# Gate/up stage of a gated FNet and GEGLU kernel: T1 streams loaded ahead of h's stores, raw weights loaded later, D product behind S3 for one token pair

## The chip, the cores and the metric

One core of a Trainium2 chip runs the kernel. The metric is the device time of one execution in microseconds (us), the median of the runs shown. A run takes 1026.12 us before the change; three runs gave 1026.1, 1026.12 and 1030.14 us. The profile is that of a further execution.

## The reference

x has 2048 tokens of 640 values. One half is an FNet layer, the real part of a Fourier transform over the hidden size and then over the sequence, written as products with cosine and sine matrices. The other half is a GEGLU feed-forward layer with 1728 hidden units. A sigmoid gate mixes the two for each token. All is float32.

```python
g = sigmoid((x * gate_w).sum(-1, keepdims=True))
a = x @ dft_hid_re.T
b = x @ dft_hid_im.T
A = dft_seq_re @ a - dft_seq_im @ b
B = (gelu(x @ w_gate) * (x @ w_up)) @ w_down
out = g * A + (1 - g) * B
```

## The kernel before

**Arithmetic.** Every float32 operand is kept as a high and a low part, so one product of two tiles is three matmuls into the same PSUM bank (`mm3`, lines 101 to 103: high by high, high by low, low by high). A split is made by ScalarE (ACT) writing the high part (line 82) and VectorE (DVE) subtracting it from the raw value for the low part (line 85). A second way of making a low part exists for x in the Fourier stage: ACT writes the negative high part (line 93), and a DMA on GpSimd's queue (POOL) adds the raw value to it in memory (`left_of`, line 97).

**Seven products.** The gate/up stage works on blocks f of 128 hidden units, f = 1 to 12, and on two token pairs, tp = 0 and 1. Products of two-by-two blocks are made with seven products instead of eight: sums of weight blocks (S1 to S4, A11, A12, A22) times sums of token blocks (T1 to T4). The hidden size of x is five tiles of 128: four go into this form, and `u5`, `g5` and `D` are the weights that meet the fifth tile of x (x1 and x2 below are its two token halves). The blocks f = 5 and 6, 7 and 8, 9 and 10, 11 and 12 also form pairs, whose A11 products are themselves shared in a seven-product form over the blocks (`together`, `together_up`). From f = 7 on (`THIRD`), S1 times T1 is shared in the same way (`together_s`): it needs three combined token streams, called xs1 to xs3 here. `pair_of(f)` is 1 for the first block of a pair and 2 for the second.

**The streams.** `sums_across("xs", ...)` makes those three streams once. `loads_s` reads four raw blocks of T1 from DRAM, on the queue of SyncE (SP). `s123` is a list of five pieces of work: sums, part 1, sums, part 2, part 3. Each part splits its sum into high and low and stores both to DRAM on POOL's queue. `load_across` loads one stream back (512 KB, on POOL's queue) for each of the blocks 7, 9 and 11. `xq` and `xu` are the like streams of the other two shared products.

**Order.** The code runs inside `in_order(PE, ACT, DVE, POOL)`: each engine executes its instructions in the order in which the code issues them. `gate_up` is a generator, one for each token pair, and the loop over `step` runs a piece of one and then a piece of the other. Behind each piece `fill` takes work off the list `fills` (weight sums and splits, token sums) by a budget of costs. So DVE and ACT hold the evictions of PSUM that TensorE waits for and the preparation of later blocks in one stream each. `make_w`, `load_w`, `make_third` and `load_third` prepare and load the weights of the next block and of the next pair; `load_third` loads the raw weights called wt. POOL's queue holds h's stores as well: `keep(hA...)` on line 456 stores the hidden values of a block, four stores for each.

**The steps concerned.** In a second block from f = 8 on, `gate_up` issues S4, S2, then the D product into bank pZ, then S3 into bank pX, then `u5` times x1 into the same bank pX, which S3's values must have left first (line 675 adds them to `s5`). Line 667 adds the bank of D to `s2`. In `f == THIRD - 2`, which is 5, the raw blocks are loaded at step 4 and three pieces of `s123` are queued at the end of `fills`; the other two follow in block 6. At step 5 of a second block stream xs2 of the next block is loaded, ahead of h's stores; xs1 and xs3 are loaded inside the next block, behind them. In block 12 the first tiles of the Fourier stage (`split_xa`, `split_c`) are prepared: x's low part by DVE for the first column piece (`sp` = 0), by DMA for the next.

Of the kernel before, what the change touches and what calls it, by code (L numbers as in the profile page):

```python
# [12 lines left out]
ALU = mybir.AluOpType  # L13
# [9 lines left out]
NF = F // P  # L23
# [6 lines left out]
THIRD = 7  # L30
# [7 lines left out]
def kernel(  # L38
# [60 lines left out]
    def mm3(ps, lhs, rhs, first, last):  # L99
        (lh, ll), (rh, rl) = lhs, rhs  # L100
        nc.tensor.matmul(ps, lh, rh, start=first, stop=False, skip_group_check=True)  # L101
        nc.tensor.matmul(ps, lh, rl, start=False, stop=False, skip_group_check=True)  # L102
        nc.tensor.matmul(ps, ll, rh, start=False, stop=last, skip_group_check=True)  # L103
# [500 lines left out]
    def gate_up(f, W, B, tp, s5, s1t, xs, s4, zs):  # L604

        n = f"{f}_{tp}"
        kind = pair_of(f)  # L610
        s_kind = kind if f >= THIRD else 0
        if s_kind == 2:
            Z = zs[f][tp]
            mm3(Z, W["u5"], at(B[5], 1), False, True)
            yield 68
            nc.scalar.activation(s5, Z, AF.Copy)
            yield
        X = bank(f"pX{n}")
        if not s_kind:
            Z = bank(f"pZ{n}")  # L620
        xs[tp] = X
        x1, x2 = at(B[5], 0), at(B[5], 1)
        k, second = divmod(f - 1, 2)

        def prod(ps, a, b, first):
            for i in range(2):
                mm3(ps, W[a, i], at(B[b], i), first and i == 0, True)

        prod(X, "A11", (1, 1), True)
        yield 136  # L630
        if not kind:
            V = bank(f"pV{n}")
            nc.scalar.activation(V, X, AF.Copy)
        else:
            s1 = s1t[kind - 1, tp] if (kind, tp) != (1, 1) else None
            if s1 is not None:
                tt(s1, s1, X, op=ALU.add)
        yield
        if not kind:
            prod(V, "A12", (2, 1), False)  # L640
            mm3(V, W["g5"], x1, False, True)
            yield 204
            s1 = mtile(F32, f"s1{n}")
            nc.scalar.activation(s1, V, AF.Gelu_apprx_tanh)
            yield
        if not s_kind:
            prod(Z, "S1", "T1", True)
            mm3(Z, W["u5"], x2, False, True)
            yield 204
            nc.scalar.activation(s5, Z, AF.Copy)  # L650
            yield
        elif s_kind == 1:
            yield 0
            yield
            Z = zs[f][tp]
        else:
            prod(Z, "S4", (2, 2), False)
            yield 136
            yield
        prod(X, "S2", "T2", False)  # L660
        yield 136
        s2 = copy(X, f"s2{n}")
        yield
        mm3(Z, W["D"], x2, False, s_kind == 2)
        yield 68
        if s_kind == 2:
            tt(s2, s2, Z, op=ALU.add)
            nc.scalar.activation(s2, s2, AF.Gelu_apprx_tanh)
        if kind:
            s1 = s1t[kind - 1, tp]  # L670
            nc.scalar.activation(s1, s1, AF.Gelu_apprx_tanh)
        yield
        prod(X, "S3", "T3", False)
        yield 136
        tt(s5, s5, X, op=ALU.add)
        yield
        if s_kind != 2:
            prod(Z, "S4", (2, 2), False)
            yield 136
            tt(s2, s2, Z, op=ALU.add)  # L680
            nc.scalar.activation(s2, s2, AF.Gelu_apprx_tanh)  # L681
            yield
        if not kind:
            prod(X, "A22", "T4", False)
        mm3(X, W["u5"], x1, False, True)
        yield 68 if kind else 204
        tt(s2, s2, s5, op=ALU.mult)  # L687
        keep(hA[tp][k], 1 + 2 * second, s2)
        if kind:
            c21 = s4[kind - 1, tp]  # L690
            tt(c21, c21, X, op=ALU.add)
            tt(s1, s1, c21, op=ALU.mult)
        else:
            tt(s1, s1, X, op=ALU.mult)
        keep(hA[tp][k], 2 * second, s1)
        if k not in STORED:
            yield
            return
        if not second:
            tt(s5, s2, s1, op=ALU.subtract)  # L700
            keep(hT[tp][k], 0, s5)
            hid[tp] = s2, s5
            yield
            return
        h12, t1 = hid.pop(tp)

        def last_sums():
            tt(h12, s2, h12, op=ALU.subtract)
            keep(hT[tp][k], 2, h12)
            tt(t1, s2, t1, op=ALU.subtract)  # L710
            keep(hT[tp][k], 1, t1)

        def last_sum():
            tt(s5, s1, t1, op=ALU.subtract)
            keep(hT[tp][k], 3, s5)

        todo.extend([(122, last_sums), (61, last_sum)])
        yield
# [641 lines left out]
    with in_order(PE, ACT, DVE, POOL):  # L1360
        for f in range(1, NF):
# [10 lines left out]
                loadp()  # L1372
                fills.extend(t123)
            if f == THIRD - 1:
                fills.extend(s123[3:])
            third = kind == 1 and f >= THIRD
            if f + 1 < NF and not third:
                nxt, work = make_w(f + 1)
                if f + 1 == THIRD:
                    ws, (sums, across, highs, lows) = make_third(f + 1)  # L1380
                    work = [sums, *work[:2], across, *work[2:4], highs, work[4], lows, *work[5:]]
                if kind != 1 or f == PAIRED:
                    fills.extend(work)
            if kind == 1 and PAIRED < f < THIRD:
                fills.extend(work)
            if f == NF - 1:
                for k in range(2):
                    fetch_xn(k)
                    load_c(k)

                def made():
                    sums_made.pop(0)()

                for k in range(2):
                    fills.extend([(126, partial(split_xa, k, not k)), (122, made), (245, partial(split_c, k))])
                fills.extend([(126, partial(split_xa, 2, False)), (0, made)])
            state.update(pe=0, done=0, all=sum(c for c, _ in fills), pe_all=2450 if not kind else (2994, 1768)[kind - 1] if f < THIRD else (3198, 1496)[kind - 1])
            s5 = pair(F32, f"s5{f}")
            xs = {}
# [11 lines left out]
                more_s = together_s(f, W, ws, s5, zs, parks)  # L1411
            for k in range(4):
                run(more)
                if third and k in (1, 3):
                    load_across(f, "xs", Ts, kepts, k)
                if third and k == 2:
                    load_w(f + 1)
                    if f + 2 < NF:
                        load_third(f + 2)
            for step in range(8 if not kind else 7):  # L1420
                if third and step == 5:
                    unpark(f + 1, zs, parks)
                for tp, w in enumerate(work):
                    run(w)
                    if third:
                        if step == 0:
                            run(more_s if not tp else more)
                        if (step, tp) == (0, 1):
                            load_across(f, "xu", Tu, keptu, 1)
                            run(more_s)  # L1430
                            load_across(f, "xu", Tu, keptu, 2)
                            run(more)
                            run(more_s)
                            run(more)
                            run(more_s)
                            load_across(f, "xu", Tu, keptu, 3)
                        elif (step, tp) == (2, 0):
                            run(more_s)
                            run(more_s)
                        elif (step, tp) == (3, 0):  # L1440
                            run(more_s)
                    elif (step, tp) in ((0, 1), (1, 1)):
                        run(more)
                        if step == 0:
                            run(more)
                    if (2, 0) < (step, tp) < (6, 0):
                        run(more_up)
# [4 lines left out]
                    for k in (1, 2, 3):  # L1452
                        load_across(f + 1, "xq", Tp, keptp, k)
                if step == 5 and pair_of(f + 1) == 1 and f + 1 >= THIRD:
                    load_across(f + 1, "xs", Ts, kepts, 2)
                if f == THIRD - 2 and step == 4:
                    loads_s()
                    fills.extend(s123[:3])
                if f == THIRD - 1 and step == 5:
                    todo.extend(s4th)  # L1460
                if step == 5 and f + 2 == THIRD:
# [1 line left out]
                if third and step == 1:  # L1463
                    nxt, parts = make_w(f + 1)
                    if f + 2 < NF:
                        ws, (sums, across, highs, lows) = make_third(f + 2)
                        parts = [*parts[:3], sums, across, *parts[3:5], highs, parts[5], lows, *parts[6:]]
                    fills.extend(parts)
                    state["all"] += sum(c for c, _ in parts)
                if step == 5 and not (f + 2 >= THIRD and pair_of(f + 2) == 2):  # L1470
# [461 lines left out]
```

## Time and profile before

| what | value |
|---|---|
| runs | 1026.1, 1026.12, 1030.14 us |
| the profiled execution | 1028.07 us |
| its span in the profile | 1026.3 us |
| granted TensorE clock, mean | 0.998 |
| TensorE matmuls, busy | 1015.4 us, 99% of the span |
| VectorE busy | 832.0 us, 81% |
| ScalarE busy | 508.8 us, 50% |
| GpSimd busy | 188.6 us, 18% |
| share of TensorE in the chain that ended last | 91% |

The profile is that of one execution. Its time, 1028.07 us, holds 1.8 us outside the span. Lines of the profile name the engine, the line of the kernel and the tiles: `pX<-x05h,wa` is a matmul that reads x05h and wa and writes bank pX. `xs<-xs` is the load of a stream, from DRAM tile xs to tile xs on the chip. A wait in square brackets ahead of an arrow says how long the engine sat idle and what released it.

### The profile page before, as it was taken

Reading aid. Unit: us, or ns where it says so; the run is one execution under the profiler, and the core shown is the slowest. Engines: PE = TensorE matmul, PEld = TensorE weight load, DVE = VectorE, ACT = ScalarE, POOL = GpSimd, SP = SyncE. Lnnn points to the kernel's source line nnn. Section 1 sums busy time; section 2 is a strip of 40 time slices with the busy share of each in tenths; the row PEclk is TensorE's granted clock in tenths of the full one; section 3 lists DMA queues with packets and bytes.
Section 4 is the critical chain, followed back from the end, with each engine's and each line's share of the span. In section 5 each row is a group of like instructions: output and inputs, shape, how many; then the busy total and the mean of one; then the engine's idle time right before and its main releaser. Section 6 shows DMA issues by size and latency. Waiting matters only on the chain.

```text
span 1026.3 us, 13389 instructions
## 1 busy us (share of the span) xinstructions
PE 1015.4 (99%) x4480; PEld 835.0 (81%) x4480; DVE 832.0 (81%) x1186; ACT 508.8 (50%) x660; POOL 188.6 (18%) x329
## 2 busy tenths in 40 slices
PE   9999999999999999999999999999999999999998
PEld 7888787787878878888888888888888888888887
DVE  8987776776856778987977897679798997997796
ACT  6644445454544764442543444434637736664340
POOL 1221232314120210032004301220111011011112
PEclk9999999999999999999999999999999999999999
DMA  9566485939596996589669966979989998997856
GB/s 351 157 210 228 167 268 188 307 135 300 161 315 215 300 244 214 195 313 381 227 202 351 352 233 224 376 259 326 338 302 384 360 387 330 350 363 213 267 143 100
DMA packets 97878, 275.46 MB, mean 268 GB/s; under 512 B 13008, under 2 KB 24912, under 8 KB 97808
## 3 DMA queue, kind: packets, MB, share of 16 engines
q1 hardware_dynamic: 68640, 182.35, 50.7%
q0 software_dynamic: 28880, 92.05, 28.5%
q8 instruction: 35, 0.57, 0.2%
q14 instruction: 35, 0.29, 0.1%
q10 hardware_dynamic: 288, 0.20, 0.1%
HBM read 199.03 MB, written 66.60 MB: 259 GB/s over the span
## 4 chain that ended last, share of the span: by engine, by line
PE 91%; DVE 3%; DMA 3%; issue 2%; ACT 1%; POOL 0%; DVEq 0%; POOLq 0%; ACTq 0%
PE pX L103 6%; PE pX L101 6%; PE pX L102 6%; PE pZ L101 4%; PE pZ L102 4%; PE pZ L103 4%; PE pL L103 3%; PE pL L102 3%; PE pL L101 3%; PE pV L101 2%; PE pV L102 2%; PE pV L103 2%; PE pR L102 1%; PE pQ L102 1%; PE pY L102 1%
## 5 line engine op out<-in xcount | busy, mean ns | idle before, releaser
L82 ACT ACTIVATE ch<-csa 128x1024 fp32r<-128x1024 f32 x32 | 34.0, 1062 | 78.2 <-DVE csa L894 72.9
L85 DVE TENSOR_TENSOR cl<-cra,ch 128x1024 fp32r<-128x1024 f32 x32 | 39.1, 1222 | 24.0 <-ACT ch L82 21.8
L82 ACT ACTIVATE ch<-cra 128x1024 fp32r<-128x1024 f32 x32 | 33.9, 1059 | 46.8 <-DVE cl L85 14.2
L85 DVE TENSOR_TENSOR cl<-crb,ch 128x1024 fp32r<-128x1024 f32 x32 | 39.1, 1222 | 16.1 <-ACT ch L82 14.7
L456 POOL DMA_DIRECT2D hA<-s x48 | 26.4, 550 | 137.0 <-DVE s L687 118.4
L103 PE MATMUL pL<-ch,xal 128*128 128x512 f32 x128 | 50.1, 392 | 0.0
L102 PE MATMUL pL<-cl,xah 128*128 128x512 f32 x128 | 50.1, 391 | 0.0
L101 PE MATMUL pL<-ch,xah 128*128 128x512 f32 x128 | 48.8, 389 | 0.0
L82 ACT ACTIVATE ch<-crb 128x1024 fp32r<-128x1024 f32 x32 | 33.8, 1056 | 29.6 <-DVE cl L85 8.5
L85 DVE TENSOR_TENSOR cl<-csa,ch 128x1024 fp32r<-128x1024 f32 x32 | 39.1, 1221 | 8.4 <-ACT ch L82 6.2
L149 ACT ACTIVATE s<-pX 128x512 f32<-128x512 f32 x41 | 24.1, 596 | 40.9 <-PE pX L103 40.0
L85 DVE TENSOR_TENSOR cl<-csb,ch 128x1024 fp32r<-128x1024 f32 x32 | 39.2, 1224 | 4.2 <-ACT ch L82 3.2
L82 ACT ACTIVATE ch<-csb 128x1024 fp32r<-128x1024 f32 x32 | 34.0, 1062 | 13.9 <-DVE csb L897 5.2
L1532 POOL DMA_DIRECT2D uA<-c x8 | 4.3, 539 | 168.1 <-DVE c L1644 167.8
L103 PEld LDWEIGHTS pL<-ch,xal 128*128 128x128 f32 x128 | 24.2, 189 | 5.1
L101 PEld LDWEIGHTS pL<-ch,xah 128*128 128x128 f32 x128 | 24.0, 188 | 5.1
L102 PEld LDWEIGHTS pL<-cl,xah 128*128 128x128 f32 x128 | 24.0, 188 | 5.0
L82 ACT ACTIVATE kh<-kw 128x1024 fp32r<-128x1024 f32 x24 | 25.5, 1063 | 5.1 <-PE kL L102 4.2
L681 ACT ACTIVATE s<-s 128x512 f32<-128x512 f32 x18 | 11.3, 633 | 32.8 <-DVE s L680 32.8
L103 PE MATMUL pX<-ch,xal 128*128 128x512 f32 x64 | 25.1, 393 | 2.2 <-DMA xal<-xn 2.2
L85 DVE TENSOR_TENSOR kl<-kw,kh 128x1024 fp32r<-128x1024 f32 x18 | 21.9, 1219 | 4.4 <-ACT kh L82 4.4
L103 PE MATMUL pZ<-ch,xal 128*128 128x512 f32 x64 | 25.4, 397 | 0.0
(3759 smaller groups left out, 3508.6 us busy)
## 6 DMA issues: line engine op xcount, KB each, us to landing
cra<-in_ct SPq DMA_DIRECT2D x64, 512.0 KB, 5.0
crb<-in_ct SPq DMA_DIRECT2D x64, 512.0 KB, 5.6
kr<-hA SPq DMA_DIRECT2D x36, 512.0 KB, 7.6
hA<-s POOLq DMA_DIRECT2D x48, 256.0 KB, 3.2
ux<-uA SPq DMA_DIRECT2D x24, 512.0 KB, 7.5
ux<-uT SPq DMA_DIRECT2D x16, 512.0 KB, 6.3
hT<-s POOLq DMA_DIRECT2D x24, 256.0 KB, 3.7
xq<-xp POOLq DMA_DIRECT2D x12, 512.0 KB, 4.7
```

The costliest lines, as they stand in the source:

```text
L82: nc.scalar.activation(hi, raw, AF.Copy)
L85: nc.vector.tensor_tensor(lo, raw, hi.bitcast(F32), op=ALU.subtract)
L101: nc.tensor.matmul(ps, lh, rh, start=first, stop=False, skip_group_check=True)
L102: nc.tensor.matmul(ps, lh, rl, start=False, stop=False, skip_group_check=True)
L103: nc.tensor.matmul(ps, ll, rh, start=False, stop=last, skip_group_check=True)
L149: nc.scalar.activation(m, src, AF.Copy)
L456: nc.gpsimd.dma_start(to[:, i], src)
L681: nc.scalar.activation(s2, s2, AF.Gelu_apprx_tanh)
L1532: nc.gpsimd.dma_start(to[:, i], src)
```

## The change

1. In block 5 the raw blocks of T1 are loaded at the start, two pieces of `s123` (sums, part 1) stand ahead of the weight work, and two (sums, part 2) behind it; block 6 keeps only part 3.
2. At step 5 of blocks 6, 8 and 10 both xs2 and xs1 of the next block are loaded; inside the next block only xs3 is.
3. `load_third(f + 2)` moves from the run ahead of the steps to step (0, 1), behind the third `xu` load.
4. The weight work of blocks 7 and 9 is queued in another order.
5. In blocks 8, 10 and 12, for tp = 1, S3 and its addition are issued ahead of the D product; tp = 0 gets empty steps so that both have eight.
6. `split_xa(1)` makes the low part by DVE, as `split_xa(0)` does; its ACT negative and its DMA on POOL's queue are gone.

```diff
@@ gate_up
         s2 = copy(X, f"s2{n}")
         yield
+        if s_kind == 2 and tp:
+            yield 0
+            yield
+            prod(X, "S3", "T3", False)
+            yield 136
+            tt(s5, s5, X, op=ALU.add)
+            yield
         mm3(Z, W["D"], x2, False, s_kind == 2)
...
-        prod(X, "S3", "T3", False)
-        yield 136
-        tt(s5, s5, X, op=ALU.add)
-        yield
+        if s_kind != 2 or not tp:
+            prod(X, "S3", "T3", False)
+            yield 136
+            tt(s5, s5, X, op=ALU.add)
+            yield
+        if s_kind == 2 and not tp:
+            yield 0
+            yield
@@ the loop over f
             if f == THIRD - 1:
-                fills.extend(s123[3:])
+                fills.extend(s123[4:])
...
+            if f == THIRD - 2:
+                loads_s()
+                work = [*s123[:2], *work, *s123[2:4]]
...
-                    fills.extend([(126, partial(split_xa, k, not k)), (122, made), (245, partial(split_c, k))])
+                    fills.extend([(126, partial(split_xa, k)), (122, made), (245, partial(split_c, k))])
...
-                if third and k in (1, 3):
-                    load_across(f, "xs", Ts, kepts, k)
+                if third and k == 1:
+                    load_across(f, "xs", Ts, kepts, 3)
                 if third and k == 2:
                     load_w(f + 1)
-                    if f + 2 < NF:
-                        load_third(f + 2)
-            for step in range(8 if not kind else 7):
+            for step in range(7 if kind and not (kind == 2 and f >= THIRD) else 8):
...
                             load_across(f, "xu", Tu, keptu, 3)
+                            if f + 2 < NF:
+                                load_third(f + 2)
...
                 if step == 5 and pair_of(f + 1) == 1 and f + 1 >= THIRD:
-                    load_across(f + 1, "xs", Ts, kepts, 2)
-                if f == THIRD - 2 and step == 4:
-                    loads_s()
-                    fills.extend(s123[:3])
+                    for k in (2, 1):
+                        load_across(f + 1, "xs", Ts, kepts, k)
...
-                        parts = [*parts[:3], sums, across, *parts[3:5], highs, parts[5], lows, *parts[6:]]
+                        parts = [*parts[:5], sums, parts[5], across, parts[6], highs, lows]
```

Line numbers behind the first edit are 7 or 11 higher in the changed kernel (a load of a stream is on line 1340 instead of 1329, line 667 becomes 674, line 675 becomes 683, or 669 in the new place).

The first place is POOL's queue where block 6 ends and block 7 begins. `hA` are h's stores, the number behind `xs_` on the right is the DRAM tile of a stream: 573 is xs1, 574 is xs2, 575 is xs3. Before:

```order
L1329 DMA xs_1824<-xs_574 128x1024
L456 DMA hA_67<-s_0_1747 128x512
L456 DMA hA_67<-s_1523 128x512
L456 DMA hA_73<-s_1_1761 128x512
L456 DMA hA_73<-s_1432 128x512
L1329 DMA xs_1863<-xs_573 128x1024
L1329 DMA xs_1888<-xs_575 128x1024
```

In the changed kernel the same place of POOL's queue reads:

```order
L1340 DMA xs_1824<-xs_574 128x1024
L1340 DMA xs_1826<-xs_573 128x1024
L456 DMA hA_67<-s_0_1753 128x512
L456 DMA hA_67<-s_1539 128x512
L456 DMA hA_73<-s_1_1768 128x512
L456 DMA hA_73<-s_1440 128x512
L1340 DMA xs_1865<-xs_575 128x1024
```

The load of xs1 moved past h's four stores; xs3 is left behind them. It is the same where block 8 ends and where block 10 ends.

The second place is VectorE at the end of block 8; pZ_0 and pZ_1 are the banks of D for tp = 0 and 1, pX_0 and pX_1 those of S3. Before:

```order
L85 TENSOR_TENSOR ws9l<-ws9r,ws9h 128x1024
L667 TENSOR_TENSOR s_0_2186<-s_0_2186,pZ_0_2068 128x512
L667 TENSOR_TENSOR s_1_2197<-s_1_2197,pZ_1_2069 128x512
L675 TENSOR_TENSOR s_2124<-s_2124,pX_0_2140 128x512
L675 TENSOR_TENSOR s_2124<-s_2124,pX_1_2151 128x512
```

In the changed kernel the same place of VectorE reads:

```order
L85 TENSOR_TENSOR ws9l<-ws9r,ws9h 128x1024
L674 TENSOR_TENSOR s_0_2186<-s_0_2186,pZ_0_2068 128x512
L683 TENSOR_TENSOR s_2124<-s_2124,pX_0_2140 128x512
L669 TENSOR_TENSOR s_2124<-s_2124,pX_1_2151 128x512
L674 TENSOR_TENSOR s_1_2197<-s_1_2197,pZ_1_2069 128x512
```

The read of bank pZ_1 moved behind both reads of pX, so one operation instead of two stands between the weight split and the first read of pX. Blocks 10 and 12 have the same rows in the same change.

The third place is TensorE in block 12, ahead of `u5` times x1 into pX_0 (`x05h`, `wa`). The tiles ch, cl and xah, xal belong to the Fourier stage. Before:

```order
L103 MATMUL pX_1_2971<-xT13h,ws12l 128x512
L101 MATMUL pZ_3116<-ch_1_2966,xah_2943 128x512
L102 MATMUL pZ_3116<-cl_1_2967,xah_2943 128x512
L103 MATMUL pZ_3116<-ch_1_2966,xal_2944 128x512
L103 MATMUL pX_3114<-ch_0_3005,xal_2986 128x512
L102 MATMUL pX_3115<-cl_0_3006,xah_2985 128x512
L103 MATMUL pX_3115<-ch_0_3005,xal_2986 128x512
L102 MATMUL pL_3120<-cl_0_3006,xah_2985 128x512
L103 MATMUL pL_3120<-ch_0_3005,xal_2986 128x512
L101 MATMUL pL_3121<-ch_0_3005,xah_2985 128x512
L102 MATMUL pL_3121<-cl_0_3006,xah_2985 128x512
```

Behind these come the last row of pL_3121 and three of pZ_3117, and then `u5`. In the changed kernel TensorE's rows from D's last matmul to `u5` are:

```order
L103 MATMUL pZ_1_2879<-x15h,wa_2801 128x512
L101 MATMUL pZ_3115<-ch_1_2966,xah_2943 128x512
L102 MATMUL pZ_3115<-cl_1_2967,xah_2943 128x512
L103 MATMUL pZ_3115<-ch_1_2966,xal_2944 128x512
L102 MATMUL pX_3114<-cl_0_3005,xah_2985 128x512
L103 MATMUL pX_3114<-ch_0_3004,xal_2986 128x512
L101 MATMUL pL_3119<-ch_0_3004,xah_2985 128x512
L102 MATMUL pL_3119<-cl_0_3005,xah_2985 128x512
L103 MATMUL pL_3119<-ch_0_3004,xal_2986 128x512
L101 MATMUL pX_0_2955<-x05h,wa_2801 128x512
```

`u5` is row 1487 of TensorE's order instead of 1493, so six matmuls of the Fourier stage that stood ahead of it are now behind it. The number of matmuls is 4496 in both orders.

## The prediction

> **What bounds the kernel now.** I read the page first: its busy times and its chain.
>
> ```profile
> PE 1015.4 (99%) x4480; PEld 835.0 (81%) x4480; DVE 832.0 (81%) x1186; ACT 508.8 (50%) x660; POOL 188.6 (18%) x329
> PE 91%; DVE 3%; DMA 3%; issue 2%; ACT 1%; POOL 0%; DVEq 0%; POOLq 0%; ACTq 0%
> ```
>
> TensorE is busy for 99% of the span, and the change leaves it the same 4496 matmuls. It can therefore only win or lose TensorE's waits and stretches of a slower clock. The waits of TensorE, summed by what ended them (us in total, times, longest), come next.
>
> ```profile
> PE pX L103 <- DMA xal<-xn: 2.2, 1, 2.2
> PE pX L101 <- DVE s L675: 1.3, 2, 0.7
> PE pX L101 <- DVE s L637: 1.0, 1, 1.0
> PE pZ L101 <- ACT s L149: 1.0, 1, 1.0
> PE pZ L101 <- DMA xs<-xs: 0.9, 1, 0.9
> ```
>
> These six waits are 6.4 us, and all lie where the change works. Third, each is sized in TensorE's timeline, as the distance of two starts less a step between matmuls. The step is 0.23 us (254.35 to 254.58 below). The columns are start, duration, engine, line, operation, and in brackets the idle time.
>
> ```profile
> 178.10 0.39 PE L103 MATMUL pZ<-x15h,wa 128*128 128x512 f32 x1
> 179.49 0.50 PE L101 MATMUL pX<-xT02h,ws6h 128*128 128x512 f32 x1 [1.00 <-DVE s L637]
> 179.82 0.39 PE L102 MATMUL pX<-xT02l,ws6h 128*128 128x512 f32 x1
> ...
> 203.24 0.39 PE L103 MATMUL pH7t<-x05h,wq7l 128*128 128x512 f32 x1
> 204.56 0.47 PE L101 MATMUL pZ<-xs,wt7h 128*128 128x512 f32 x1 [0.93 <-DMA xs<-xs]
> ...
> 237.38 0.39 PE L103 MATMUL pX<-xT13h,ws8l 128*128 128x512 f32 x1
> 238.43 0.50 PE L101 MATMUL pX<-x05h,wa 128*128 128x512 f32 x1 [0.67 <-DVE s L675]
> ...
> 252.65 0.39 PE L103 MATMUL pH9t<-x05h,wq9l 128*128 128x512 f32 x1
> 254.04 0.47 PE L101 MATMUL pZ<-xs,wt9h 128*128 128x512 f32 x1 [1.00 <-ACT s L149]
> 254.35 0.40 PE L102 MATMUL pZ<-xs,wt9h 128*128 128x512 f32 x1
> 254.58 0.40 PE L103 MATMUL pZ<-xs,wt9l 128*128 128x512 f32 x1
> ...
> 358.64 0.39 PE L102 MATMUL pX<-cl,xah 128*128 128x512 f32 x1
> 361.21 0.50 PE L103 MATMUL pX<-ch,xal 128*128 128x512 f32 x1 [2.18 <-DMA xal<-xn]
> ```
>
> The step that follows a wait is longer too (179.49 to 179.82, 0.33 for 0.23), so a wait costs 0.1 more than its gap. Block 6: 1.39 less 0.23, and 0.10, is **1.26**. Block 7: 1.32 less 0.23, and 0.08, is **1.17**. Block 8: 1.05 less 0.23, and 0.1, is 0.92, and block 10 the same, as the second of the two waits on line 675. Block 9: 1.39 less 0.23, and 0.08, is **1.24**. Block 12, where x's low part is waited for: 2.57 less 0.23, and 0.1, is **2.44**. Block 9's wait is booked on ACT, but its matmul reads stream xs1 as the one in block 7 does, whose wait ended with that load; I take it for the load.
>
> Last I looked at the clock behind the longest wait. The windows table has busy times, then the granted clock, the DMA share and GB/s.
>
> ```profile
> 354.00:358.00 4.00, 4.00 (x20) 3.30 (x19) 3.50 (x6) 3.30 (x5) 0.64 (x1) 1.00 1.04 330
> ...
> 362.00:366.00 4.00, 4.00 (x12) 3.12 (x11) 3.47 (x6) 3.34 (x4) 0.87 (x1) 0.57 1.05 331
> ```
>
> From 362 to 366 the clock was 0.57, so 0.43 of 4 us, **1.7 us**, was lost on top of the wait. The same page's mean clock, 0.998 of 1026 us, leaves room for about one such stretch (2 us). The DMA share is above 1 throughout: transfers there stand in each other's way.
>
> **The change part by part.** *Streams made in block 5 (edit 1).* VectorE before, in block 5 and ahead of block 6's wait, and a piece of the chain there:
>
> ```profile
> 159.87 0.69 DVE L85 TENSOR_TENSOR wa<-wa6r,wa 128x512 fp32r<-128x512 f32 x1 [2.77 <-ACT wa L82]
> 163.56 0.69 DVE L675 TENSOR_TENSOR s<-s,pX 128x512 f32<-128x512 f32 x1 [3.00 <-PE pX L103]
> 165.60 0.69 DVE L675 TENSOR_TENSOR s<-s,pX 128x512 f32<-128x512 f32 x1 [1.35 <-PE pX L103]
> ...
> 177.55 1.28 DVE L85 TENSOR_TENSOR xs<-xs,xs 128x512 fp32r<-128x512 f32 x2
> 178.76 0.68 DVE L637 TENSOR_TENSOR s<-s,pX 128x512 f32<-128x512 f32 x1
> ...
> 174.41 2.83 DMA wt7b<-in_wf
> ```
>
> Line 637 reads the bank that S2 writes next, and stands behind the stream work, four sums and three low parts. In the new order one low part is left ahead of line 637, and six operations of 0.68 at most, 4.1 us, move into block 5, where VectorE idles 7.1 us in the three rows. In their place one operation, line 277 on the raw weights wt7a and wt7b, moves ahead of line 637. If wt7b lands as late as before, at 177.24, line 637 ends at 177.24 + 0.60 + 0.68 = 178.5, 0.2 behind S2's turn (178.10 + 0.23); otherwise well ahead of it. I take **1.26**, all of block 6's wait, with 0.3 less as the other end. The cover is block 5's idle time; without it, each 0.7 us of VectorE ahead of the evictions on line 675 would show. The four raw loads move with the work, ahead of block 6's weights on SP's queue, and the two stores of xs1 on POOL's go ahead of the `xu` loads. No row shows these waits. If the four 256 KB reads at the 330 GB/s of the windows above (3.2 us) hit a load that is just in time, they cost at most those 3.2 us; below nothing is excluded, as nothing waits there now. I take 0, since the idle rows there end on TensorE and ACT and not on a load.
>
> *xs1 ahead of h's stores (edit 2).* POOL before, and the chain's piece:
>
> ```profile
> 189.37 0.55 POOL L1329 DMA_DIRECT2D xs<-xs  x1 [0.99 <-DVE s L675]
> 194.96 0.54 POOL L456 DMA_DIRECT2D hA<-s  x1 [0.83 <-DVE s L692]
> 195.57 1.16 POOL L1329 DMA_DIRECT2D xs<-xs  x2
> 195.57 8.85 DMA xs<-xs
> 206.72 0.39 PE L101 MATMUL pH7s<-xs,wt7h 128*128 128x512 f32 x1
> ```
>
> The load of xs1 was issued at 195.57, behind stores that wait for VectorE's last results, and flew 8.85 us, to 204.42. Behind xs2 it can go at 189.37 + 0.55 = 189.92. With the same flight it lands at 198.8, and is needed at 203.24 + 0.23 = 203.47. 4.7 us of room also cover a later free buffer. So **1.17** goes, and in block 9, the same wait at the same place of its block, **1.24**. What is late next is xs3: still issued behind the stores, second of the pair at 195.57, landed at 205.0 with the same flight, used at 206.72. TensorE comes to that matmul earlier by the 1.26 and 1.17, at 204.3. Its load has no xs1 beside it now, 0.5 MB or 1.5 us at 330 GB/s, so I take 203.5 and no wait; with the old flight it is 0.7 late.
>
> *S3 before D (edit 5).* VectorE before, in block 8:
>
> ```profile
> 236.50 1.28 DVE L667 TENSOR_TENSOR s<-s,pZ 128x512 f32<-128x512 f32 x2
> 237.70 1.28 DVE L675 TENSOR_TENSOR s<-s,pX 128x512 f32<-128x512 f32 x2
> ```
>
> The matmul at 238.43 waits for the first line 675 (237.70 and 0.68). One of the two operations ahead moves behind, and they start 0.60 apart, so the wait shrinks from 0.92 to 0.32: **0.60** in block 8 and **0.60** in block 10. D's bank is read 1.2 later, but its consumers are ACT and h's stores, which nothing on TensorE awaits here.
>
> *x's low part by VectorE (edit 6), and six matmuls behind `u5`.* The rows of block 12:
>
> ```profile
> 333.97 1.04 ACT L93 ACTIVATE xal<-xn 128x1024 fp32r<-128x1024 f32 x1
> 335.99 1.23 DVE L85 TENSOR_TENSOR cl<-cra,ch 128x1024 fp32r<-128x1024 f32 x1 [3.02 <-ACT ch L82]
> 344.63 0.69 DVE L691 TENSOR_TENSOR s<-s,pX 128x512 f32<-128x512 f32 x1 [1.93 <-PE pX L103]
> 349.39 1.06 ACT L82 ACTIVATE xah<-xn 128x1024 fp32r<-128x1024 f32 x1 [3.51 <-DVE xn L860]
> 351.81 9.35 DMA xal<-xn
> ```
>
> ACT loses 1.04, VectorE gains 1.22 inside an idle 3.02: nothing on the path. One accumulating DMA of 512 KB goes. The transfer that TensorE waits for is two pieces further; its ACT work waited for VectorE (3.51), and VectorE for `u5` (1.93 idle ahead of 344.63). `u5` now stands six matmuls, 6 x 0.23 = 1.4 us, earlier. So the transfer starts at 350.4 instead of 351.81 and with 9.35 lands 1.4 earlier. Its flight should shrink by up to the 1.5 that a half megabyte takes; I count 0.6, because the share stays above 1. Of 2.44, **2.0** goes, between 1.0 (ACT's step alone) and all.
>
> *The clock.* Behind block 9's wait, 1.24, TensorE keeps the step of 0.23 (254.35 to 254.58), so a rest of 0.4 should not start a low clock: **1.7** goes. The Trainium skill's page "TensorE: Matmul & The Clock Gate", section "HAM oscillation — how this bites in real kernels", states the rule "no PE-idle gaps >~3.4µs". By it a wait of 2.18 would not have cost the clock, and the sum would lack this 1.7; the trace has the low clock right behind that wait, so I follow the trace.
>
> *Edits 3 and 4*, weight loads and pieces moved: no wait of TensorE is on them now. Between nothing and, where a moved load is late, a wait like the xs rows, 1.2; I take 0.
>
> **Sum.** 1.26 + 1.17 + 1.24 + 0.60 + 0.60 + 2.0 + 1.7 = 8.6. Against the profiled execution's own 1028.07 that is 1019.5. The runs' median is 1.95 lower; if that is the stretch of low clock missing there, the sum is 6.9 from 1026.1, 1019.2. I predict **1019.5**.
>
> **The rivals.** *Low part still late.* If the 3.51 idle moves little and the flight stays, 1.0 is won and the low clock stays: 1028.07 − 4.87 − 1.0 = **1022.2**. For it speak the DMA share above 1; against it the six matmuls.
>
> *xs1 doesn't come earlier.* If it still waits for a buffer or an earlier DMA until h's stores are out, blocks 7 and 9 keep 2.4: **1021.9**. Against it, xs2 left at 189.37 through the same queue.
>
> *The clock stays for another reason*, as by the page's rule: without the 1.7, **1021.2**.
>
> *Slower: xs3 takes xs1's place.* In blocks 7, 9 and 11 the one load left behind the stores would meet the moved raw weights on full DMA engines. At 0.7 late it gives back 0.7 in two or three blocks: 1021.0 to 1021.6. From about 2 us late on (landing past 206.3 in block 7) the low clock joins, as in block 12: 2.44 + 1.7 = 4.1 in each of three blocks, 12.4 in all, **1031.9**. The flight of 8.85 at full share speaks for it, the load's unchanged place and lighter company against.
>
> **How the numbers follow.** The sum 0.52; low part late 0.17; xs1 not earlier 0.07; clock kept 0.07; xs3 mildly late 0.09; xs3 heavily late 0.08. Low end: all of blocks 8, 10 and 12, and the median's base with the low clock in it, 1026.1 − 9.6 = 1016.5. High end: the mild cases and half of the heavy one, 1026.5. A measurement of this kernel can tell about 0.5% (5.1 us): faster is below 1021.0, slower above 1031.3. The sum's case gives 0.50 to faster, and a quarter of the mild ones 0.12; the heavy case is slower: faster 0.62, same 0.30, slower 0.08.
>
> **What would show it.** Right: TensorE's list of waits without line 637, without xs loads, two waits of about 0.3 behind line 683, and a clock of 1.00 near 362. Wrong: a wait on xs or on wt in the first blocks of pairs, a wait in block 5 or 6 on the loads that moved, or a wait for xal of 1.4 and more with a clock below 1 behind it.

## The result, and the profile after

| | before | changed |
|---|---|---|
| median of the runs | 1027.36 us | 1019.19 us |
| lowest to highest, 4 runs each | 1026.1 to 1030.14 | 1018.72 to 1019.66 |
| the profiled execution | 1028.07 | 1019.31 |
| its span | 1026.3 | 1017.5 |
| mean granted clock | 0.998 | 1.0 |

The ratio of the runs is 0.9917, with a 95% interval of 0.9893 to 0.9941: the changed kernel is faster by 0.8%. The forecast was 1019.5 us. Before's runs scatter by 4 us and the changed kernel's by 1 us; with the runs of later comparisons before's medians were 1027.88, 1026.4 and 1027.53.

The page of the changed kernel, and its list of TensorE's waits (line waiting, what ended the wait, us in total, times, longest):

```profile
PE 1013.0 (100%) x4480; PEld 835.2 (82%) x4480; DVE 834.3 (82%) x1187; ACT 508.2 (50%) x659; POOL 187.7 (18%) x328
PE idle L1158 <- PEq L1932: 0.8, 1, 0.8
```

The five kinds of wait that filled the list before are all gone from it. What stays is 0.8 us at the very start, which stood there before as well. TensorE's timeline at the same places:

```profile
178.68 0.39 PE L103 MATMUL pZ<-x15h,wa 128*128 128x512 f32 x1
178.91 0.39 PE L101 MATMUL pX<-xT02h,ws6h 128*128 128x512 f32 x1
...
202.52 0.40 PE L103 MATMUL pH7t<-x05h,wq7l 128*128 128x512 f32 x1
202.76 0.39 PE L101 MATMUL pZ<-xs,wt7h 128*128 128x512 f32 x1
...
235.34 0.39 PE L103 MATMUL pZ<-x15h,wa 128*128 128x512 f32 x1
235.79 0.50 PE L101 MATMUL pX<-x05h,wa 128*128 128x512 f32 x1
236.13 0.40 PE L102 MATMUL pX<-x05l,wa 128*128 128x512 f32 x1
...
250.01 0.40 PE L103 MATMUL pH9t<-x05h,wq9l 128*128 128x512 f32 x1
250.25 0.39 PE L101 MATMUL pZ<-xs,wt9h 128*128 128x512 f32 x1
...
354.00 0.39 PE L102 MATMUL pX<-cl,xah 128*128 128x512 f32 x1
354.22 0.39 PE L103 MATMUL pX<-ch,xal 128*128 128x512 f32 x1
```

In blocks 6, 7, 9 and 12 the two starts are one step (0.23 us) apart, so the waits are nothing. In block 8 they are 0.45 apart and the next 0.34: 0.22 and 0.11 are left of 0.92. The windows table where the low clock was (busy times, granted clock, DMA share, GB/s):

```profile
354.00:358.00 4.00, 4.00 (x19) 3.34 (x18) 3.49 (x6) 3.33 (x4) 0.87 (x1) 1.00 1.01 251
358.00:362.00 4.00, 4.00 (x20) 3.30 (x19) 3.93 (x7) 3.03 (x4) 0.00 (x0) 1.00 1.06 278
```

The clock is 1.00 although the DMA share is as high as before. The changed kernel's execution lost a little elsewhere. The second of TensorE's matmuls into pg, on loads that the change doesn't touch, before and then after:

```profile
5.29 0.41 PE L102 MATMUL pg<-x011l,w0h 128*128 128x512 f32 x1
```

```profile
5.88 0.62 PE L102 MATMUL pg<-x011l,w0h 128*128 128x512 f32 x1
```

It began 0.59 later (5.88 for 5.29). In the other kernels below, the same matmul starts between 0.28 earlier and 0.41 later than in the kernel before. So spans that differ by less than about 0.9 are not told apart here; waits are.

### The profile page after: what moved, and what is told of

Same layout as the page of the kernel before. It is cut to its first block, busy times and chain, and to the rows that moved or that the text cites. A ratio compares the mean times of both kernels' runs of the same rounds, so it can differ in the third digit from the quotient of the medians.

```text
span 1017.5 us, 13384 instructions
## 1 busy us (share of the span) xinstructions
PE 1013.0 (100%) x4480; PEld 835.2 (82%) x4480; DVE 834.3 (82%) x1187; ACT 508.2 (50%) x659; POOL 187.7 (18%) x328
## 4 chain that ended last, share of the span: by engine, by line
PE 98%; DVE 1%; issue 0%; ACT 0%; ACTq 0%
PE pX L101 7%; PE pX L103 7%; PE pX L102 7%; PE pZ L101 4%; PE pZ L103 4%; PE pZ L102 4%; PE pL L101 3%; PE pL L102 3%; PE pL L103 3%; PE pV L101 2%; PE pV L102 2%; PE pV L103 2%; PE pY L101 1%; PE pR L101 1%; PE pQ L101 1%; PE pY L102 1%
## 5 line engine op out<-in xcount | busy, mean ns | idle before, releaser
L102 PE MATMUL pX<-cl,xah 128*128 128x512 f32 x64 | 24.9, 389 | 0.0
```

## The experiments

Each kernel has a profile and times of its own, and is compared by TensorE's waits. A wait is the distance of two starts less 0.23, without the slower step behind it. A transfer's flight is the time from its issue to its landing.

**Edit 6 undone.** x's second low part by ACT and DMA again.

```diff
-fills.extend([(126, partial(split_xa, k)), (122, made), (245, partial(split_c, k))])
+fills.extend([(126, partial(split_xa, k, not k)), (122, made), (245, partial(split_c, k))])
```

> The changed kernel with x's second low part made by ACT's negative and the accumulating DMA again. In TensorE's order `u5` of block 12 then stands 3 matmuls later than in the changed kernel and 4 earlier than before. If the transfer taken away is what helped (shorter flight of the third accumulate, 7.1 us instead of 9.4), the flight is back at 9 us or more and TensorE waits for xal by 1.4 to 2.1 us. If the earlier `u5` alone helped, 0.9 us of its 1.4 is kept and the flight doesn't matter: a wait of 1.4 to 1.6 with a flight that may be short. If neither matters (the wait was an accident of one execution), no wait, span 1017.5. A wait of 1.4 or more followed by a granted clock near 0.57 for 3.4 us would add 1.7: span 1020.6 to 1021.4; without the low clock 1018.9 to 1019.6.

Measured: 1021.38 us (1020.1 to 1023.83, 6 runs), ratio to before 0.9946 [0.993, 0.9963], span 1019.7, clock 1.0. TensorE's waits, its timeline at them, and the transfer in the chain:

```profile
PE pX L103 <- DMA xal<-xn: 1.8, 2, 1.4
```

```profile
346.81 0.39 PE L102 MATMUL pX<-cl,xah 128*128 128x512 f32 x1
347.59 0.50 PE L103 MATMUL pX<-ch,xal 128*128 128x512 f32 x1 [0.39 <-DMA xal<-xn]
...
354.34 0.39 PE L102 MATMUL pX<-cl,xah 128*128 128x512 f32 x1
356.17 0.50 PE L103 MATMUL pX<-ch,xal 128*128 128x512 f32 x1 [1.45 <-DMA xal<-xn]
```

```profile
347.86 8.27 DMA xal<-xn
```

The wait is back, 1.60 us (356.17 less 354.34 less 0.23), and a second one of 0.55 stands one piece earlier. So edit 6 is worth 2.2 us of waits here, and the medians differ by as much. No low clock followed in the profiled execution. Of the other five executions two show a mean clock of 0.998 and spans of 1021.5 and 1022.1, the rest 0.999 or 1.0 and 1018.3 to 1019.5, so this kernel, too, seems to lose the clock in some executions. The flight was 8.27, a little shorter than the 9.35 of before and longer than the 7.1 of the changed kernel. The transfer also left late: ACT had finished that piece at 345.6, and POOL issued it at 347.86, just after the second piece had let TensorE go on at 347.59. The trace doesn't show what held it for those 2.2 us, and this stays open.

**Edit 5 undone.** D ahead of S3 for both token pairs.

```diff
-        if s_kind == 2 and tp:
...
-            prod(X, "S3", "T3", False)
...
-        if s_kind != 2 or not tp:
-            prod(X, "S3", "T3", False)
+        prod(X, "S3", "T3", False)
...
-            for step in range(7 if kind and not (kind == 2 and f >= THIRD) else 8):
+            for step in range(8 if not kind else 7):
```

> The changed kernel with D ahead of S3 for both token pairs. My sum: the waits of blocks 8 and 10 on the read of pX grow by 0.6 us each (0.84 and 0.76 by the lead of the changed kernel's matmuls), span 1018.7 to 1019.1, and xal is not waited for, as its transfer starts 0.6 earlier and flies 2.3 shorter than before. Rival, the order of TensorE in block 12 carries xal's gain: `u5` is back by 3 matmuls, 0.7 us, and TensorE waits for xal by 1 to 1.7 us, with or without a low clock behind it: span 1020 to 1022.

Measured: 1021.93 us (1021.18 to 1022.57, 4 runs), ratio 0.9950 [0.9931, 0.9968], span 1020.5, clock 0.999. Its waits and the transfer in its chain:

```profile
PE pX L101 <- DVE s L675: 1.3, 2, 0.7
PE pX L103 <- DMA xal<-xn: 1.3, 1, 1.3
```

```profile
347.27 8.99 DMA xal<-xn
```

Blocks 8 and 10 have their waits of before. (A further wait of 0.5, on the load of kl near 800 us, is in a later stage that the change doesn't touch.) My sum had missed the third effect: TensorE waits for xal by 1.5 us, though its DMA for the second piece is gone. The ACT timeline of this kernel, and then of the changed one, shows a change of order that goes with it (line 668 here is 675 there, the gelu of a token pair; lines 82 and 93 split x):

```profile
336.32 0.63 ACT L668 ACTIVATE s<-s 128x512 f32<-128x512 f32 x1 [0.80 <-DVE s L667]
...
337.38 1.04 ACT L82 ACTIVATE xah<-xn 128x1024 fp32r<-128x1024 f32 x1
338.32 1.04 ACT L93 ACTIVATE xal<-xn 128x1024 fp32r<-128x1024 f32 x1
```

```profile
334.97 1.06 ACT L82 ACTIVATE xah<-xn 128x1024 fp32r<-128x1024 f32 x1
335.94 1.04 ACT L93 ACTIVATE xal<-xn 128x1024 fp32r<-128x1024 f32 x1
337.08 0.64 ACT L675 ACTIVATE s<-s 128x512 f32<-128x512 f32 x1
```

With D behind S3, the second pair's gelu moves behind the split of x in ACT's stream, and the transfer ahead of the awaited one leaves at 337.41 instead of 339.80, 2.4 us earlier, of which 0.7 is TensorE's own lead at that place. The awaited one flew 7.1 us in the changed kernel and 9.0 here. I had seen the six matmuls but not this change of ACT's order. That the order shortens the flight is not shown: the transfer ahead flew 7.0 us here and so had landed at 346.8, before the awaited one left at 347.27.

**Edit 2 undone.** xs1 behind h's stores again.

```diff
-                if third and k == 1:
-                    load_across(f, "xs", Ts, kepts, 3)
+                if third and k in (1, 3):
+                    load_across(f, "xs", Ts, kepts, k)
...
-                    for k in (2, 1):
-                        load_across(f + 1, "xs", Ts, kepts, k)
+                    load_across(f + 1, "xs", Ts, kepts, 2)
```

> The changed kernel with xs1 loaded behind h's stores again. My sum: waits for xs1 in blocks 7 and 9 return, 1.2 us each, span 1019.9. Rival, TensorE's earlier arrival makes them longer, since the load leaves when h's stores do and not when TensorE is ready: the 1.2 of block 6 and the 0.8 of block 8 add to them only if the stores don't move with TensorE; then 2.0 to 2.5 each, perhaps with a low clock, span 1021 to 1024. Rival, other edits (the sums in block 5, the later raw weights) had already taken the load off the path: no wait, 1017.5.

Measured: 1019.31 us (1018.81 to 1019.51, 4 runs), span 1017.6: no difference that these runs show. Block 7 has no wait at all. Block 9 has this:

```profile
249.42 0.39 PE L103 MATMUL pH9t<-x05h,wq9l 128*128 128x512 f32 x1
250.29 0.47 PE L101 MATMUL pZ<-xs,wt9h 128*128 128x512 f32 x1 [0.49 <-ACT s L579]
```

That is 0.64 us, not 2.4 in two blocks. My sum failed here as far as this kernel goes: something else in the change had taken most of these waits as well. The next three runs look for it.

**Edits 3 and 4 undone, edit 2 kept.** `load_third` ahead of the steps again, and the old order of the weight work.

```diff
-                            if f + 2 < NF:
-                                load_third(f + 2)
...
                     load_w(f + 1)
+                    if f + 2 < NF:
+                        load_third(f + 2)
...
-                        parts = [*parts[:5], sums, parts[5], across, parts[6], highs, lows]
+                        parts = [*parts[:3], sums, across, *parts[3:5], highs, parts[5], lows, *parts[6:]]
```

> The changed kernel with edits 3 and 4 undone: raw weights of the next pair loaded ahead of the steps, and the weight work in its old order; xs1 stays early. If the early load is enough by itself, as my sum had it, no wait in blocks 7 and 9, span 1016.9 to 1017.6. Rival: the later raw weights are what freed the transfers; then xs3, or the streams of the other products, wait by 0.5 to 1.5 us in blocks 7 and 9: 1018 to 1020.

Measured: 1020.16 us (1019.38 to 1021.81, 4 runs), span 1018.5. No wait on any xs. A wait of 0.47 on VectorE (line 587) comes in block 9, and one of 0.28 on xal. So the early load is enough for xs1 by itself. The median is 1.0 above the changed kernel's, of which these two waits are 0.75. In block 7, xs3 landed at 204.31 here and was used at 204.56, so it was just in time.

**Edits 2, 3 and 4 undone.** Both diffs together.

> The changed kernel with edits 2, 3 and 4 undone, so that xs1 leaves behind h's stores and the raw weights ahead. With edit 2 alone undone the waits for xs1 were 0 in block 7 and 0.65 in block 9. If edits 3 and 4 had shortened that load's flight (7.7 for 8.9 us in block 7), both waits come back to about 1.1 and 1.2 less what the stores won: 1.5 to 2.4 in all, span 1018.4 to 1019.4. If edits 3 and 4 don't matter and the stores leave earlier for another reason (less work on VectorE in block 6), the waits stay at 0 and 0.65: span 1017.5.

Measured: 1021.83 us (1020.59 to 1022.49, 4 runs), span 1019.6. The waits list, and the load of xs1 in block 7, in a view of the DMAs issued near 193.9 (KB each, us to landing):

```profile
PE pZ L101 <- DMA xs<-xs: 1.7, 2, 0.9
```

```profile
xs<-xs POOLq DMA_DIRECT2D x1, 512.0 KB, 9.4
```

The waits are back, 0.99 and 1.03. With only edit 2 undone, the same load flew

```profile
xs<-xs POOLq DMA_DIRECT2D x1, 512.0 KB, 7.7
```

So by these traces either of edit 2 and the pair of edits 3 and 4 alone takes most of the waits for xs1, and the ratios to the kernel before go the same way: 0.9924 with edit 2 undone and 0.9939 with edits 3 and 4 undone, 0.9952 here. Edit 2 does it by an earlier issue. For edits 3 and 4 a shorter flight fits, but it is hardly clear of the scatter. Behind the stores xs1 flew 8.0 to 9.4 us in blocks 7 and 9 of the three kernels with neither edit (this one, the kernel before, and the one with edits 5 and 6 alone). It flew 7.5 to 8.0 in the kernel with both edits and in the one with edit 4 alone.

**Edits 2 and 3 undone, 4 kept.** The first diff of `load_third` and that of `load_across`.

> The changed kernel with edits 2 and 3 undone, edit 4 kept. With 2, 3 and 4 undone the waits for xs1 were 1.0 and 1.0; with only 2 undone 0 and 0.65. If the later raw weights (edit 3) had shortened xs1's flight, the waits are about 1.0 and 1.0 here and the flight in block 7 is about 9.4 us. If the order of the weight work (edit 4) did it, they are 0 and 0.65 and the flight is about 7.7.

Measured: 1020.52 us (1020.16 to 1021.32, 4 runs), span 1019.5. Block 7 has no wait and a flight of 7.5 us, block 9 a wait of 1.00, and xal one of 0.58. That fits neither answer in both blocks, and which of edits 3 and 4 matters stays open. The flights scatter too, as the next run shows.

**Edits 5 and 6 alone**, on the kernel of before.

> The kernel of before with edits 5 and 6 alone. If these two carry everything in blocks 8, 10 and 12, the waits left are line 637 (1.2), xs1 in blocks 7 and 9 (1.0 to 1.2 each) and 0.23 in blocks 8 and 10; xal is not waited for or by 0.3 at most, and the clock is 1.0: span 1020.5 to 1021.1. Rival, the earlier edits matter for xal too (less traffic or earlier work upstream): a wait for xal of 1 us or more, span above 1021.5.

Measured: 1023.47 us (1022.04 to 1023.6, 5 runs), ratio 0.9956 [0.9938, 0.9974], span 1020.2, clock 1.0. The profiled execution, 1022.04, is the fastest of the five by 1.0. Beside line 637's, its list has the wait of block 9:

```profile
PE pZ L101 <- ACT s L149: 1.0, 1, 1.0
```

Nothing waits for xal, and no low clock follows: the two edits carry block 12 alone. Line 637 and block 9's xs1 wait as before (1.17 and 1.20). In block 7 the wait is 0.22, though nothing about the streams was changed there. So one trace tells a wait that ends on a load here only to about 1 us.

**Edit 1 undone.** The streams read and summed where they were before.

```diff
-            if f == THIRD - 2:
-                loads_s()
-                work = [*s123[:2], *work, *s123[2:4]]
...
+                if f == THIRD - 2 and step == 4:
+                    loads_s()
+                    fills.extend(s123[:3])
```

> The changed kernel with the streams' raw blocks loaded at the end of block 5 and their sums made there and in block 6 as before. My sum: the wait on line 637 in block 6 returns, 1.2 us, nothing else, span 1018.7. Rival, the early streams are what lets xs1 and xs2 load early in block 7: a wait for xs1 or xs2 in block 7 as well, span 1019.9 or more.

Measured: 1020.07 us (1019.94 to 1020.18, 4 runs), span 1018.3, and one wait of note:

```profile
PE pX L101 <- DVE s L637: 1.0, 1, 1.0
```

It is 1.17 us, as in the kernel before, and nothing else came back. Edit 1 is worth block 6's wait and no more.

**S3 ahead of D for both token pairs**, to take what is left in blocks 8 and 10.

```diff
-        if s_kind == 2 and tp:
-            yield 0
-            yield
+        if s_kind == 2:
...
-            for step in range(7 if kind and not (kind == 2 and f >= THIRD) else 8):
+            for step in range(7 if kind else 8):
```

> The changed kernel with S3 ahead of D for both token pairs, without the empty steps. The first read of pX then has no read of D's bank ahead of it, and the last waits of blocks 8 and 10, 0.23 each and 0.1 behind each, go: span 0.5 to 0.7 less than the changed kernel's with the same start, 1016.2 to 1017.0. Rival: the D banks, read later, hold up S4 or the next block's bank by as much: no difference, or up to 1 us more. `u5` of block 12 is one matmul earlier still, so xal is not waited for.

Measured: 1019.97 us (1019.5 to 1020.84, 5 runs), span 1018.2. The two waits of 0.23 went, and waits of 0.58 in block 9 on line 587 and of 0.28 on xal came. It isn't better than the changed kernel.

**The clock, measured by itself.** The changed kernel with more work for VectorE ahead of S3's eviction, to make TensorE wait longer; in the second probe `EXTRA` is `{2: 8, 4: 8, 6: 10, 8: 4, 10: 4}`.

```diff
+    EXTRA = {2: 6, 3: 5, 4: 7, 6: 8, 8: 2, 9: 6, 10: 3, 12: 5}
...
+                for _ in range(0 if tp else EXTRA.get(f, 0)):
+                    tt(gwb[:, 0:T], gwb[:, 0:T], gwb[:, 0:T], op=ALU.max)
```

> The changed kernel with idle work put into VectorE's stream in blocks 2, 3, 4, 6, 8, 9, 10 and 12: 6, 5, 7, 8, 2, 6, 3 and 5 operations of 0.6 us that rewrite a tile with its own values, ahead of the first read of pX's S3. TensorE gets waits of different lengths, up to about 4.5 us, each counted by its gap. By the page's rule (low clock only behind an idle time over 3.4 us) only waits near or above 3.4 are followed by steps of 0.43 us. By what the profile of before showed (a wait of 2.2 followed by low clock, waits of 1.0 to 1.6 not) the border lies between 1.6 and 2.2, so that waits of 2.2 to 3.4 are followed too. If the border depends on when the wait falls, some waits of 2 to 3.4 are followed and others are not.

Each probe was run once, at 1041.67 and 1045.42 us. TensorE's timeline of the first:

```profile
143.05 0.39 PE L103 MATMUL pZ<-x122h,ws4l 128*128 128x512 f32 x1
145.84 0.50 PE L101 MATMUL pX<-x05h,wa 128*128 128x512 f32 x1 [2.40 <-DVE s L686]
...
294.73 0.39 PE L103 MATMUL pZ<-x15h,wa 128*128 128x512 f32 x1
297.24 0.50 PE L101 MATMUL pX<-x05h,wa 128*128 128x512 f32 x1 [2.12 <-DVE s L686]
...
297.81 0.63 PE L103 MATMUL pX<-x05h,wa 128*128 128x512 f32 x1
298.24 0.63 PE L101 MATMUL pX<-x15h,wa 128*128 128x512 f32 x1
```

And the windows of the same kernel behind both waits:

```profile
148.00:152.00 4.00, 4.00 (x19) 3.31 (x18) 3.93 (x7) 2.40 (x5) 1.67 (x4) 1.00 0.36 137
297.79:301.20 3.41, 3.41 (x9) 2.65 (x8) 3.31 (x6) 1.25 (x3) 1.02 (x2) 0.50 0.86 320
```

The longer wait, 2.56 us at 145.84, kept the full clock. The shorter one, 2.28 at 297.24, was followed by steps of 0.43 until 301.2. Waits of 2.05, 1.99 and 1.56 kept the clock, and one of 3.41 was followed by low clock. So the length alone doesn't decide.

> The same probe with 8, 8, 10, 4 and 4 operations in blocks 2, 4, 6, 8 and 10, for waits of 2.3 to 3.4 us. In the first probe waits of 2.28 and 3.41 were followed by low clock, 2.05, 1.99 and 2.56 not. If a wait's length alone decides, all of 2.6 and more are followed. If a free-running window of 3.41 us decides, the first low stretch gives the grid of the windows, and a wait is followed exactly where some window of the grid was idle for more than 0.6 of it: waits of 2.3 to 3.4 that straddle a border with less than 2 us on either side are not.

Its waits came out longer than meant, at 3.50, 3.26, 3.45, 3.01 and 3.01 us, and all five were followed by low clock (mean clock 0.99). Three of the five stretches, by the windows:

```profile
94.24:97.65 3.41, 3.41 (x10) 2.67 (x9) 2.90 (x8) 1.33 (x3) 0.00 (x0) 0.50 0.00 1
148.85:152.26 3.41, 3.04 (x7) 2.46 (x8) 3.31 (x6) 1.23 (x2) 0.10 (x1) 0.50 0.25 90
305.87:312.69 6.82, 6.04 (x14) 4.79 (x15) 6.58 (x14) 1.73 (x3) 2.12 (x4) 0.50 0.62 235
```

The stretches of low clock ended at 97.7, 152.3, 206.9, 258.1 and 312.7 us. The distances, 54.6, 54.6, 51.2 and 54.6, are 16, 16, 15 and 16 times 3.413 us. In the first probe the ends at 301.2 and 379.7 are 78.5 apart, 23 times 3.413. If a grid of 3.413 is laid through those ends, the window of the 2.28 wait was idle for 0.67 of it, and that of the wait of 2.34 in the kernel of before for 0.65. The 2.56 wait was cut by a border into 0.27 and 0.48. Windows idle for 0.51 and less, all waits within one added, were not followed; those of 0.65 and more were. Two stretches lasted two windows: there the wait ran on for 0.67 and 0.77 us into the low clock, and for 0.37 or less where one window was all.

## Why the prediction was right

The sum was 8.6 us against the profiled execution; the span fell by 8.8 (1026.3 to 1017.5). By its terms:

| term | predicted | measured |
|---|---|---|
| block 6, line 637 | 1.26 | 1.26, all gone |
| block 7, xs1 | 1.17 | 1.16 |
| block 9, xs1 | 1.24 | 1.23 |
| blocks 8 and 10, line 675 | 0.60 each | 0.59 and 0.58 |
| block 12, xal | 2.0 | 2.44, all gone |
| low clock behind it | 1.7 | gone, 1.6 to 1.7 |
| later start, not foreseen | | -0.6 |

These add to 8.3 or 8.4; the rest of 0.4 or 0.5 lies in single steps that I haven't assigned. That the total agrees to 0.2 is in part luck: xal's term came out 0.4 larger, and the later start took 0.6 back. The measure is the forecast's, a gap less a step and the slower step behind it.

*Block 6* is shown: with edit 1 undone its wait returned whole and alone. Line 277, the new neighbour, cost nothing.

*Blocks 8 and 10* are shown by edit 5 undone. One operation instead of two ahead of the eviction was the whole of it.

*xs1.* The size was right and the mechanism only half told. In the changed kernel the load left at 188.77 and stores followed, as the POOL timeline has it. It landed at 195.4, 7.4 us ahead of its use.

```profile
188.77 0.54 POOL L1340 DMA_DIRECT2D xs<-xs  x1 [0.95 <-PE pZ L103]
190.33 0.55 POOL L456 DMA_DIRECT2D hA<-s  x1 [1.01 <-DVE s L698]
194.18 0.55 POOL L1340 DMA_DIRECT2D xs<-xs  x1
```

Block 9's wait was the load's, as I had taken it: before, the load landed at 253.91 and the matmul began at 254.04, and no kernel that loads xs1 early has this wait. Edit 2 is enough, as the run with 3 and 4 undone shows. It isn't needed for all of it: with edit 2 undone 1.7 of the 2.4 stayed won. The prediction priced edits 3 and 4 at nothing because no wait ended on the transfers they move. In block 7 the load behind the stores had 7.9 us from issue to need before, and 8.5 in each of the three kernels with edit 2 undone; a flight of 9.4 made the wait in one of them, flights of 7.7 and 7.5 made none in the others. That edits 3 and 4 shorten the flight, by moving the transfers beside it, is argued from this and not shown.

*xs3*, the rival's load, was on time, and no kernel here has a wait on it. It landed at 203.52, as forecast, but by luck: I had taken 1.5 off its flight, and that hardly shrank (9.47 before):

```profile
xs<-xs POOLq DMA_DIRECT2D x1, 512.0 KB, 9.3
```

It left 2.0 earlier instead (194.18 for 196.18), as the stores ahead of it moved with TensorE, which is 1.9 earlier there. It was 1.3 ahead of its use. With edits 3 and 4 undone it flew 10.4 and was 0.25 ahead, so by that one trace the rival was nearer than a price of 0 for these edits says.

*xal.* The term was 0.4 too small, and its parts were off. The start came 1.2 earlier against TensorE's own time (346.00 for 351.81, at a TensorE that is 4.64 earlier there), 1.4 was predicted. The flight was 7.1 for 9.35, so 2.25 shorter where I took 0.6:

```profile
xal<-xn POOLq DMA_DIRECT2D x1, 512.0 KB, 7.1
```

Both edits are needed, by the waits: with edit 6 undone they were 0.55 and 1.60, with edit 5 undone 1.5, and in the eight kernels that have both, 0 to 0.58. The medians agree, 2.2 and 2.7 above the changed kernel's, the second with 1.2 from blocks 8 and 10. One part of this is the time from the transfer's issue to TensorE's need: 7.1 us before, 6.7 with edit 6 undone, 7.6 with edit 5 undone, and 8.2 to 8.5 in all eight with both. That part I had foreseen. The other part is the flight, and it scatters. In the eight kernels it was 6.4 to 8.8 us, here in the one with edit 1 undone and the one with edits 2 and 3 undone:

```profile
xal<-xn POOLq DMA_DIRECT2D x1, 512.0 KB, 6.4
```

```profile
xal<-xn POOLq DMA_DIRECT2D x1, 512.0 KB, 8.8
```

With one edit undone it was 8.3 and 9.0. So the flight shrank by 0.6 to 3.0 with both edits; that it was 2.25 in the changed kernel's profile is one draw, and my 0.6 the lower end. What shortens it, the transfer that goes, the ACT order that I had not seen, or another, stays open.

*The clock.* The 1.7 went with the wait, as forecast, and the rival with a low clock for another reason fell. But the ground was too simple: a rest below the length of block 9's wait. The probes show that the place of the wait in a window of 3.41 us counts. So the wait of 2.34 need not cost the clock in every execution, and the record bears this out. Of the 26 executions of the kernel before that stand beside the experiments, 10 have a mean clock of 0.998, as the profiled one has, and a median of 1028.2 us; the other 16 have 0.999 or 1.0, and 1026.3. The 1.9 between them is about one stretch of low clock. It is luck that the profiled execution had one; the others fit the forecast's second sum, 1019.2 from 1026.1.

The heavy rival, xs3 late in three blocks, did not come about, and its price is not tested.

## What to carry to other kernels

Where TensorE is busy for 99%, a list of its single waits, each priced from two starts and the next step, gives the gain of an edit to a few tenths. What a wait on a load will do is known less well than a wait on an engine. Two edits can each take the same wait, so undo each by itself, and both together, before naming the one that did it. And split such a wait into the time from issue to need, which the order sets, and the flight: the first was the same to 0.3 us in eight kernels here, the second differed by 2.4.

## What the runs showed of the hardware

The granted clock went to half (0.50) for whole stretches of 3.41 us, or two of them, whose ends lie on a grid of 3.413 us in one execution. It did so where a window of that grid had been idle for 0.65 and more, not at 0.51 and less. A wait of 2.28 us cost it and one of 2.56 didn't. The Trainium skill's page "TensorE: Matmul & The Clock Gate", section "🔬 Part 1: The HAM clock gate (the "warmup" mystery)", tells of a free-running activity window of 4096 cycles, about 3.4 us; the distances of the ends agree with it. The rule "no PE-idle gaps >~3.4µs" of the same page's section "HAM oscillation — how this bites in real kernels" allows too much by these runs: waits of 2.28 and 2.34 us cost the clock.
